# Pooled attention and two MLPs on one core: sums and conversions held in program order, the first attention along the weight fold, y from other tiles

## The chip, the cores and the metric

The kernel runs on one core of one Trainium2 chip. Its engines are TensorE (PE in the profile; PEld is its weight load), VectorE (DVE), ScalarE (ACT), GpSimd (POOL) and SyncE (SP), each working through its own stream of instructions in order. The metric is the time of one execution on the device in microseconds; the median of three runs counts.

## The reference

All inputs of the two MLPs are float64 words in DRAM, q, k and v are float32. What is computed, cut to what matters:

```python
# attention: 8 batches, 8 heads, 576 tokens, 64 wide; k and v averaged over 8 tokens
k_p = k.reshape(B, H, 72, 8, D).mean(axis=3)
v_p = v.reshape(B, H, 72, 8, D).mean(axis=3)
attn = softmax(q @ k_p.T / sqrt(D))
x = (attn @ v_p) as (4608 tokens, 512)
# first MLP (512 -> 1024 -> 1024 -> 512)
x = ((x @ w1) * (x @ w2)) @ w3 @ w_out
# second MLP (512 -> 1536 -> 512), after a norm
xn = x / sqrt(mean(x * x) + 1e-6) * rms_g
y = (silu(xn @ w_gate) * (xn @ w_val)) @ moe2_w_out
```

## The kernel before

The 4608 tokens are handled in nine blocks of 512 (index i), the attention in eight batches of 576 tokens (index b), so that a batch ends inside a block. Matrix products run as three passes over a high and a low part of each operand (`mm3`, L104 to L106; `split`, L100 and L101).

The program has these stages. First the **fold**: w3 · w_out of the first MLP is multiplied out once. Sixteen steps n, each with four transposes of a block of w3 (L553), ScalarE's copy of the transposed block into `hl` (L555) and four products (L622). The float64 words are turned into float32 by a `Conv`: a load (`s0`), then ScalarE takes the low word (L143) and, if `on_act`, the high one (L145), VectorE shifts it (L154), merges the sign (L159) and adds the two (L167). `conv.run` issues conversion steps up to a count; each step of the fold calls it for the next block, two steps more than needed. Within the fold, the attention of batch 0 and the first products `ab(0, m, s)` are called from a list `aux` that a `Ticker` spreads over the products behind number `AUX_FROM`.

Then come seven more batches of attention beside the products `ab` of blocks 0 to 8 (x·w1, copied by ScalarE at L567, times x·w2 by VectorE at L570) and beside `gv_prep`, which converts the weights of the second MLP into sums of blocks (L774) and high and low parts (`wst`, L100 and L101), stored by POOL (L791). `positions(b)` lays the steps of a batch over sixteen places: place 1 the load of the next batch's k (`k0`), 8 the sum of v, 9 the next batch's loads of v, 13 the products with v, 14 the sum of the next batch's k (`k1`), 15 its transpose (`kT`, L282) and first q transposes (L301). `pool_four` loads half of each group of 8 tokens by SP (L243) and lets POOL's DMA add the other half (L244); `pool_sum` adds the four that are left on VectorE (L248, then L251). Scores are L319, their maximum L331 on VectorE, the exponential L334 on ScalarE, the division L345 to L347 on VectorE; the transposes of the result go over TensorE (L369) in the first two batches and over VectorE (L362) in the others; the product with v is L422, and its high and low parts are written by L429 (ScalarE) and L430 (VectorE, `xl`).

Behind them the products with the folded matrix give y; `y_end` squares y (L700), copies it into a tile `yc` (L703, L705) for the store to DRAM (L706) and adds the squares (L708, split at L714 and L716) for the norm. The second MLP (`gv`, g·silu at L1015 to L1019, x scaled in `xprep`, L1051) and its last products into `y`, `o` fill the rest.

The code is written in one order, but a scheduler places each engine's instructions by its own estimate of their times, within what data and buffers allow. So an engine's stream can differ from the program. Tiles come from rings: `ftile` has five, `hxtile("hh")` and `hxtile("hl")` two each; a ring's next tile waits for the last use of the one that it takes over. The functions that the change touches:

Of the kernel before, what the change touches and what calls it, by code (L numbers as in the profile page):

```python
# [9 lines left out]
F32 = mybir.dt.float32  # L10
# [4 lines left out]
ALU = mybir.AluOpType  # L15
# [6 lines left out]
def kernel(  # L22
# [86 lines left out]
    class Conv:  # L109
# [19 lines left out]
        def s1(self):  # L129
# [13 lines left out]
            nc.scalar.activation(self.low, low_u, AF.Copy, scale=2.0**-29)  # L143
            if self.on_act:
                nc.scalar.activation(self.tmp.bitcast(F32), hi_f, AF.Copy, scale=2.0**-112)  # L145
            else:
                nc.vector.tensor_scalar(
                    out=self.tmp.bitcast(F32),
                    in0=hi_f,
                    scalar1=2.0**-112,  # L150
                    scalar2=None,
                    op0=ALU.mult,
                )
            nc.vector.tensor_scalar(  # L154
                out=self.tmp, in0=self.tmp, scalar1=3, scalar2=None, op0=ALU.logical_shift_left
            )

        def s2(self):
            nc.vector.scalar_tensor_tensor(  # L159
                out=self.low,  # L160
                in0=self.hiw,
                scalar=-(2**31),
                in1=self.low,
                op0=ALU.bitwise_and,
                op1=ALU.bitwise_or,
            )
            nc.vector.tensor_tensor(out=self.out, in0=self.tmp, in1=self.low, op=ALU.add)  # L167
# [79 lines left out]
    def pool_sum(dst, r):  # L247
        nc.vector.tensor_tensor(  # L248
            out=r[:, :, : 2 * D], in0=r[:, :, : 2 * D], in1=r[:, :, 2 * D :], op=ALU.add
        )  # L250
        nc.vector.tensor_tensor(  # L251
            out=dst,
            in0=r[:, :, :D].rearrange("s (p j) d -> s p j d", j=2),
            in1=r[:, :, D : 2 * D].rearrange("s (p j) d -> s p j d", j=2),
            op=ALU.add,
        )
# [280 lines left out]
    def load_w3(n):  # L537
        g, j = divmod(n, KF1)

        def keep(f):  # L540
            w3r[n] = f

        src = w3.rearrange("(g i p) c -> g p i c", g=2, p=P)[g, :, :, j * P : (j + 1) * P]
        return Conv(src, praw, then=keep)
# [4 lines left out]
    def tr_w3(n):  # L549
        ps = psum()  # L550
        r = w3r.pop(n)
# [44 lines left out]
    first = {5: [A.k0], 6: [A.load_v], 7: [lambda: A.q(0)], 8: [lambda: A.q(1)]}  # L596
# [5 lines left out]
    aux += [atts[1].k0, atts[1].load_v, lambda: atts[1].q(0)]  # L602
    for m in range(4):
        aux += [lambda m=m: ab(0, m, 0), c1a[m], lambda m=m: ab(0, m, 1)]
    aux += c1a[4:]
    aux += [atts[1].k1, lambda: atts[1].q(1)]
    AUX_FROM = 38
    tick = Ticker(aux, 4 * NW3 - AUX_FROM)
    conv.run(upto[0] + 2)
    tr_w3(0)  # L610
    wps = None
    for n in range(NW3):
        g, j = divmod(n, KF1)
        if n + 1 < NW3:
            conv.run(upto[n + 1] + 2)
# [23 lines left out]
    tick.flush()  # L639
    nc.sync.dma_start(out=g_col, in_=rms_g.rearrange("(k p) -> p k", p=P))  # L640


    def y_end(i):
        ys = yacc.pop(i)
        sq = []
        for kk in range(KD):
            sq.append(ftile())
            nc.scalar.activation(sq[kk], ys[kk], AF.Square)
            yc = ftile()
            if kk % 2:  # L650
                nc.scalar.copy(yc, ys[kk])
            else:
                nc.vector.tensor_copy(yc, ys[kk])
            nc.sync.dma_start(out=ydram[i, kk], in_=yc)
            if kk:
                nc.vector.tensor_tensor(out=sq[0], in0=sq[0], in1=sq[kk], op=ALU.add)

        sp = []

        def sq_split():  # L660
            sp.append(ftile(F32R))
            nc.scalar.copy(sp[0], sq[0])
            sp.append(ftile(F32R))
            nc.vector.tensor_tensor(
                out=sp[1], in0=sq[0], in1=sp[0].bitcast(F32), op=ALU.subtract
            )

        def rms():
            ps = psum()
            nc.tensor.matmul(ps[:1], ones, sp[0], start=True, stop=False)  # L670
            nc.tensor.matmul(ps[:1], ones, sp[1], start=False, stop=True)
            row = ftile()
            nc.scalar.copy(row[:1], ps[:1])
            nc.sync.dma_start(out=sdram[i : i + 1], in_=row[:1])
            ss = const.tile([P, 4], F32, tag="ss", name="ss", bufs=2)
            nc.sync.dma_start(out=ss, in_=sdram[i].rearrange("(p c) -> p c", p=P))
            nc.vector.tensor_scalar(
                out=ss, in0=ss, scalar1=1.0 / DM, scalar2=1e-6, op0=ALU.mult, op1=ALU.add
            )
            nc.gpsimd.tensor_tensor(out=ss, in0=ss, in1=mhalf, op=ALU.pow)  # L680
            nc.sync.dma_start(out=rdram[i].rearrange("(p c) -> p c", p=P), in_=ss)

        return [sq_split, lambda: None, rms]

    def y_mm(i, m):
        c = m % 4
        second(i, m, wph[m // 4][:, c, :], wpl[m // 4][:, c, :], KF1 - 1, False)
        return y_end(i) if m == KF1 - 1 else []
# [6 lines left out]
    def y_end(i):  # L695
        ys = yacc.pop(i)
        sq = []
        for kk in range(KD):
            sq.append(ftile())
            nc.scalar.activation(sq[kk], ys[kk], AF.Square)  # L700
            yc = ftile()
# [323 lines left out]
    def xprep(i0):  # L1025
# [21 lines left out]
        def norm(j, u):  # L1047
            for k in range(2):
                z = q[f"A{j + 1}{u + 1}"][:, k * TB : (k + 1) * TB]
                kk = 2 * u + k  # L1050
                nc.vector.scalar_tensor_tensor(  # L1051
                    out=z,
                    in0=z,
                    scalar=g_col[:, kk : kk + 1],
                    in1=rr["r"][:, j * TB : (j + 1) * TB],
                    op0=ALU.mult,
                    op1=ALU.mult,
# [301 lines left out]
```

## Time and profile before

| What | us |
|---|---|
| median of three runs | 1726.54 |
| lowest, highest | 1725.12, 1729.22 |
| the profiled execution | 1726.03 |
| its span | 1724.3 |
| TensorE busy | 1622.2 |
| VectorE busy | 1012.9 |
| ScalarE busy | 679.7 |
| POOL busy | 95.0 |

The span is what the profile covers of the execution; the remaining 1.7 us lie around it. A line of waits names the engine and line that waited, what it waited for, the time in all, how many waits, and the longest. A line of the timeline gives the start, the duration, the engine and its instruction, and in brackets the idle time ahead of it with what ended it. PEclk is the share of TensorE's full clock that was granted.

### The profile page before, as it was taken

The page shows a single profiled execution, that of the slowest core. Times are in us where ns is not written, and L with a number is a line of the kernel's source. Part 1 is how long each engine was busy: PE and PEld are TensorE (multiplying, and loading weights), DVE is VectorE, ACT ScalarE, POOL GpSimd, SP SyncE. Part 2 cuts the span into 40 slices and gives each one's busy share as a digit, 9 for nine tenths or more (in the row PEclk, how much of TensorE's full clock was granted, in tenths as well). Part 3 has the DMA queues.
Part 4 walks back from the last instruction along what each step waited for, and adds up shares of the span by engine and source line. Part 5 has one row for each costly group of instructions (what it writes and reads, how often), then busy time and mean ns, then how long its engine had stood idle before and what let it go on. Part 6 is the DMA issues. An engine that isn't in the chain of part 4 may idle for free.

```text
span 1724.3 us, 20001 instructions
## 1 busy us (share of the span) xinstructions
PE 1622.2 (94%) x7250; PEld 1295.7 (75%) x7250; DVE 1012.9 (59%) x1773; ACT 679.7 (39%) x1607; POOL 95.0 (6%) x107
## 2 busy tenths in 40 slices
PE   6787997897988999999998999999999999999999
PEld 3445776675866778888876888888888888888887
DVE  6565586886967941566483242567354744465344
ACT  5675543444444431455441133333333333234322
POOL 0101011011011010001000000000000000000000
PEclk9898998998989999999999999999999999999999
DMA  8958447475574256577655664547454745455431
GB/s 244 255 138 207 122 125 180 150 172 156 151 176 156 98 189 244 194 251 255 210 202 192 228 259 169 195 183 266 149 220 169 272 182 193 160 208 197 183 109 74
DMA packets 147461, 322.53 MB, mean 187 GB/s; under 512 B 52505, under 2 KB 79129, under 8 KB 129442
## 3 DMA queue, kind: packets, MB, share of 16 engines
q1 hardware_dynamic: 126210, 276.13, 47.4%
q0 software_dynamic: 21152, 45.12, 10.0%
q8 instruction: 57, 0.93, 0.2%
q14 instruction: 42, 0.34, 0.1%
HBM read 247.75 MB, written 73.44 MB: 186 GB/s over the span
## 4 chain that ended last, share of the span: by engine, by line
PE 72%; DMA 11%; DVE 10%; issue 6%; ACT 1%; POOL 1%; SPq 1%; POOLq 0%; DVEq 0%; ACTq 0%
PE ps L104 14%; PE ps L106 14%; PE ps L105 14%; DMA kv<-in_k_dram 5%; PE o L106 5%; PE o L105 5%; PE o L104 5%; DVE aT L362 5%; PE y L104 4%; PE y L106 4%; PE y L105 4%; DMA kv<-in_v_dram 3%; PE pa L319 1%; DMA q<-in_q_dram 1%; PE wps L622 1%
## 5 line engine op out<-in xcount | busy, mean ns | idle before, releaser
L104 PE MATMUL ps<-xf,wr 128*128 128x512 f32 x576 | 224.2, 389 | 0.0
L105 PE MATMUL ps<-xf,wr 128*128 128x512 f32 x576 | 224.1, 389 | 0.0
L106 PE MATMUL ps<-xf,wr 128*128 128x512 f32 x576 | 224.1, 389 | 0.0
L106 PE MATMUL o<-oh,hcl 128*128 128x512 f32 x384 | 149.5, 389 | 0.0
L105 PE MATMUL o<-ol,hch 128*128 128x512 f32 x384 | 149.4, 389 | 0.0
L104 PE MATMUL o<-oh,hch 128*128 128x512 f32 x384 | 149.4, 389 | 0.0
L1117 ACT COPY f<-ps 128x512 f32<-128x512 f32 x144 | 84.4, 586 | 161.8 <-PE ps L106 158.6
L362 DVE STREAM_TRANSPOSE aT<-s 32x256 f32<-32x256 f32 x324 | 140.8, 435 | 4.5
L104 PEld LDWEIGHTS ps<-xf,wr 128*128 128x128 f32 x576 | 108.1, 188 | 23.0 <-ACT f L1117 0.4
L105 PEld LDWEIGHTS ps<-xf,wr 128*128 128x128 f32 x576 | 108.1, 188 | 22.5
L106 PEld LDWEIGHTS ps<-xf,wr 128*128 128x128 f32 x576 | 108.1, 188 | 22.2
L104 PE MATMUL ps<-xh,w1h 128*128 128x512 f32 x288 | 123.6, 429 | 1.0 <-ACT w1h L100 1.0
L1121 DVE TENSOR_TENSOR f<-y,f 128x512 f32<-128x512 f32 x48 | 33.2, 691 | 144.4 <-PE y L106 144.4
L334 ACT ACTIVATE s<-pa,mx 128x72 f32<-128x72 f32 (+1 forms) x280 | 85.3, 331 | 82.7 <-DVE mx L331 82.6
L105 PE MATMUL ps<-xl,w1h 128*128 128x512 f32 x288 | 116.5, 404 | 0.0
L106 PE MATMUL ps<-xh,w1l 128*128 128x512 f32 x288 | 116.1, 403 | 0.2 <-DVE w1l L101 0.2
L104 PE MATMUL ps<-xh,w2h 128*128 128x512 f32 x288 | 113.9, 396 | 2.1 <-DVE hh L570 1.8
L106 PE MATMUL ps<-xh,w2l 128*128 128x512 f32 x288 | 112.3, 390 | 0.0
L105 PE MATMUL ps<-xl,w2h 128*128 128x512 f32 x288 | 112.0, 389 | 0.0
L1203 DVE TENSOR_TENSOR acc<-o,acc 128x512 f32<-128x512 f32 x64 | 43.5, 689 | 75.5 <-PE o L106 75.0
L1141 ACT CAST hch<-f 128x512 fp32r<-128x512 f32 x72 | 44.8, 622 | 99.9 <-DVE f L1135 99.9
L106 PEld LDWEIGHTS o<-oh,hcl 128*128 128x128 f32 x384 | 72.1, 188 | 15.3 <-DVE hcl L1143 0.6
(194 smaller groups left out, 3268.9 us busy)
## 6 DMA issues: line engine op xcount, KB each, us to landing
wr<-wd SPq DMA_DIRECT2D x96, 1024.0 KB
wd<-wst POOLq DMA_DIRECT2D x48, 512.0 KB, 5.6
hr<-hd SPq DMA_DIRECT2D x36, 512.0 KB
oh<-od SPq DMA_DIRECT2D x15, 1024.0 KB
ol<-od SPq DMA_DIRECT2D x15, 1024.0 KB
wr<-wd SPq DMA_DIRECT2D x24, 512.0 KB
x1raw<-in_moe_w_dram SPq DMA_DIRECT2D x20, 512.0 KB
hd<-hh SPq DMA_DIRECT2D x40, 256.0 KB
```

What stands on the lines that cost most here:

```text
L104: nc.tensor.matmul(o, lh, rh, start=first, stop=False, skip_group_check=part)
L105: nc.tensor.matmul(o, lh, rl, start=False, stop=False, skip_group_check=part)
L106: nc.tensor.matmul(o, ll, rh, start=False, stop=last, skip_group_check=part)
L319: nc.tensor.matmul(ps[:n, (p % 2) * 2 * SP : (p % 2 + 1) * 2 * SP], qT_t[t // 2][:, t % 2, p, :n], kT[:, p, :], start=True, stop=True,)
L334: nc.scalar.activation(s_t[t][:n, h, :SP], pv[:, j, :], AF.Exp, bias=mx[:, j, :], accum_out=den_t[t][:n, h, :],)
L362: nc.vector.transpose(aT[32 * kb : 32 * kb + 32, :, s0 + 32 * i : s0 + 32 * i + 32], s_t[t][32 * i : 32 * i + 32, :, 32 * kb : 32 * kb + 32],)
L622: nc.tensor.matmul(wps[i], wt[:, i * P : (i + 1) * P], wo[j // 4][:, j % 4, :], start=j == 0, stop=j == KF1 - 1,)
L1117: nc.scalar.copy(t, bank)
L1121: nc.vector.tensor_tensor(out=t, in0=bank, in1=t, op=ALU.add)
L1141: nc.scalar.copy(hi, hf)
L1203: nc.vector.tensor_tensor(out=a, in0=ys[j], in1=a, op=ALU.add)
```

## The change

Four things change.

1. `tc.keep_in_program_order` is put around four instructions: the first addition of `pool_sum`, ScalarE's low word of a conversion (L143), VectorE's merge (L159) and the scaling of x in `xprep` (L1051). Such an instruction is placed behind the instruction that stood ahead of it on its engine in the program; no wait is added. The shift (second half of L154) is called behind the merge.
2. The blocks of w3 are read through their `Conv` instead of a callback, and the fold asks for one conversion step ahead instead of two.
3. Batch 0's loads are called at the fold's steps 0 to 3 instead of 5 to 8, its attention from product 18 on instead of 38, and `ab(0, 0..3)` with their conversions behind the fold (`tail`).
4. `y_end` copies y into `hh` and `hl` tiles. (An earlier, overwritten copy of `y_end` and `y_mm` is deleted as well.)

```diff
-            nc.scalar.activation(self.low, low_u, AF.Copy, scale=2.0**-29)
+            tc.keep_in_program_order(
+                nc.scalar.activation(self.low, low_u, AF.Copy, scale=2.0**-29)
+            )
...
+        def s2(self):
+            tc.keep_in_program_order(
+                nc.vector.scalar_tensor_tensor(
+                    out=self.low,
...
+            )
             nc.vector.tensor_scalar(
                 out=self.tmp, in0=self.tmp, scalar1=3, scalar2=None, op0=ALU.logical_shift_left
             )
...
     def pool_sum(dst, r):
-        nc.vector.tensor_tensor(
-            out=r[:, :, : 2 * D], in0=r[:, :, : 2 * D], in1=r[:, :, 2 * D :], op=ALU.add
+        tc.keep_in_program_order(
+            nc.vector.tensor_tensor(
+                out=r[:, :, : 2 * D], in0=r[:, :, : 2 * D], in1=r[:, :, 2 * D :], op=ALU.add
+            )
         )
...
-        return Conv(src, praw, then=keep)
+        w3r[n] = Conv(src, praw)
+        return w3r[n]
...
-        r = w3r.pop(n)
+        r = w3r.pop(n).out.bitcast(F32)
...
-    first = {5: [A.k0], 6: [A.load_v], 7: [lambda: A.q(0)], 8: [lambda: A.q(1)]}
+    first = {0: [A.k0], 1: [A.load_v], 2: [lambda: A.q(0)], 3: [lambda: A.q(1)]}
...
+    tail = [c1a[0]]
     for m in range(4):
-        aux += [lambda m=m: ab(0, m, 0), c1a[m], lambda m=m: ab(0, m, 1)]
-    aux += c1a[4:]
-    aux += [atts[1].k1, lambda: atts[1].q(1)]
-    AUX_FROM = 38
+        tail += [lambda m=m: ab(0, m, 0), c1a[m + 1], lambda m=m: ab(0, m, 1)]
+    tail += [c1a[5], atts[1].k1, lambda: atts[1].q(1)]
+    AUX_FROM = 18
...
-            conv.run(upto[n + 1] + 2)
+            conv.run(upto[n + 1] + 1)
...
     tick.flush()
+    for st in tail:
+        st()
...
-            yc = ftile()
+            yc = hxtile("hh" if kk % 2 else "hl").bitcast(F32)
...
-                nc.vector.scalar_tensor_tensor(
-                    out=z,
...
+                tc.keep_in_program_order(
+                    nc.vector.scalar_tensor_tensor(
+                        out=z,
```

Where instructions stand now is shown at three places. The first is VectorE's stream where batch 5 begins (`kv_3305` is a half of the k of batch 6, `xl5_3259` the low part of block 5's x, `vp_3559` the summed v, the 128x320 piece being the first). Before:

```order
L570 TENSOR_TENSOR hl_3256<-ps_3243,f_3241 128x512
L248 TENSOR_TENSOR kv_3305<-kv_3305 72x4x128
L430 SCALAR_TENSOR_TENSOR xl5_3259<-pa_3260,xh5_3258 128x320
L430 SCALAR_TENSOR_TENSOR xl5_3259<-pa_3265,xh5_3258 128x320
L430 SCALAR_TENSOR_TENSOR xl5_3259<-pa_3270,xh5_3258 128x320
L251 TENSOR_TENSOR vp_3559<-kv_3032 72x256
L430 SCALAR_TENSOR_TENSOR xl5_3259<-pa_3275,xh5_3258 128x320
L331 TENSOR_REDUCE mx_3283<-pa_3280 128x4
L331 TENSOR_REDUCE mx_3283<-pa_3297 128x4
L251 TENSOR_TENSOR vp_3559<-kv_3035 72x256
L159 SCALAR_TENSOR_TENSOR rawp_3454<-rawp_3454 128x512
L251 TENSOR_TENSOR kv_3305<-kv_3305 72x2x128
```

And now, where the sum of the same tile stands (the 128x192 pieces are the last of the block; the four 128x320 pieces stand some 60 rows ahead, with no sum of `kv_3305` beside them):

```order
L574 TENSOR_TENSOR hl_3704<-ps_3691,f_3680 128x512
L436 SCALAR_TENSOR_TENSOR xl5_3259<-pa_3706,xh5_3258 128x192
L436 SCALAR_TENSOR_TENSOR xl5_3259<-pa_3711,xh5_3258 128x192
L436 SCALAR_TENSOR_TENSOR xl5_3259<-pa_3716,xh5_3258 128x192
L436 SCALAR_TENSOR_TENSOR xl5_3259<-pa_3721,xh5_3258 128x192
L253 TENSOR_TENSOR kv_3305<-kv_3305 72x4x128
L168 TENSOR_SCALAR f_3688<-f_3688 128x512
L257 TENSOR_TENSOR kv_3305<-kv_3305 72x2x128
L253 TENSOR_TENSOR kv_3308<-kv_3308 72x4x128
L574 TENSOR_TENSOR hh_3765<-ps_3752,f_3740 128x512
L257 TENSOR_TENSOR kv_3308<-kv_3308 72x2x128
```

The sum of `kv_3305` moved from ahead of block 5's first xl to behind its last one.

The second place is TensorE's stream in the fold, around the fold's eighth to eleventh block (L553 a block's transposes, L622 its products, L282 and L301 the first of batch 0's attention). Before:

```order
L553 MATMUL ps<-ident,f 128x128 x4
L622 MATMUL wps<-wo,hl 128x512 x4
L553 MATMUL ps<-ident,f 128x128 x4
L622 MATMUL wps<-wo,hl 128x512 x4
L553 MATMUL ps<-ident,f 128x128 x4
L622 MATMUL wps<-wo,hl 128x512 x4
L553 MATMUL ps<-ident,f 128x128 x4
L622 MATMUL wps<-wo,hl 128x512
L282 MATMUL ps<-ident,kv 128x72 x4
L301 MATMUL ps<-ident,q 128x128 x4
```

And now, around the sixth and seventh block (L557, L626, L288, L307 and L325 are the L553, L622, L282, L301 and L319 of before):

```order
L557 MATMUL ps<-ident,f 128x128 x4
L626 MATMUL wps<-wo,hl 128x512 x4
L288 MATMUL ps<-ident,kv 128x72 x2
L307 MATMUL ps<-ident,q 128x128 x4
L288 MATMUL ps<-ident,kv 128x72 x2
L307 MATMUL ps<-ident,q 128x128 x4
L626 MATMUL wps<-wo,hl 128x512
L557 MATMUL ps<-ident,f 128x128 x4
L325 MATMUL ps<-kT,qT 128x144 x2
L307 MATMUL ps<-ident,q 128x128 x4
L626 MATMUL wps<-wo,hl 128x512
L325 MATMUL ps<-kT,qT 128x144 x2
```

Attention's first transposes moved from behind the eleventh block to behind the sixth.

The third place is VectorE's stream where the second MLP's products begin, with what each instruction waits for (L1016 and L1019 the steps of silu, L716 the low part of the squares' sum, `hl<-f,hh` the low part for the last products). Before:

```order
L1016 TENSOR_TENSOR f<-ps,f 128x512 [waits Activation_49]
L1016 TENSOR_TENSOR f<-ps,f 128x512 [waits DMAHW0_49,Activation_49]
L716 TENSOR_TENSOR f<-f 128x512 [waits DMAHW6_49,DMAHW4_49,Activation_49]
L1019 TENSOR_TENSOR f<-ps,f 128x512 [waits DVE_49,PE_49] x2
L101 TENSOR_TENSOR hl<-f,hh 128x512 [waits Activation_49] x2
L1016 TENSOR_TENSOR f<-ps,f 128x512 [waits Activation_49] x2
```

And now (L975, L675 and L978 are the L1016, L716 and L1019 of before):

```order
L975 TENSOR_TENSOR f<-ps,f 128x512 [waits Activation_49]
L975 TENSOR_TENSOR f<-ps,f 128x512 [waits DMAHW0_49,Activation_49]
L675 TENSOR_TENSOR f<-f 128x512 [waits PE_49,Activation_49]
L978 TENSOR_TENSOR f<-ps,f 128x512 [waits DVE_49,PE_49]
L101 TENSOR_TENSOR hl<-f,hh 128x512 [waits DMAHW1_49,Activation_49]
L978 TENSOR_TENSOR f<-ps,f 128x512 [waits PE_49]
L101 TENSOR_TENSOR hl<-f,hh 128x512 [waits DMAHW4_49,Activation_49]
```

L716's wait for two DMA queues is gone, the split into `hl` has one each, and the scaling of x moved behind this place.

## Rows read from the trace of the kernel before

**Rows 1.** The page, section 1: busy us, share of the span, instructions.
```profile
PE 1622.2 (94%) x7250; PEld 1295.7 (75%) x7250; DVE 1012.9 (59%) x1773; ACT 679.7 (39%) x1607; POOL 95.0 (6%) x107
```

**Rows 2.** Windows: stretch, length, busy PE, PEld, DVE, ACT, POOL; clock, DMA, GB/s.
```profile
0.00:63.00 63.00, 43.88 (x121) 21.03 (x122) 40.49 (x78) 35.01 (x59) 7.29 (x14) 0.97 0.90 245
63.00:148.00 85.00, 72.32 (x300) 45.49 (x299) 54.05 (x105) 54.42 (x159) 4.96 (x4) 0.92 0.66 182
148.00:604.00 456.00, 396.82 (x1955) 315.91 (x1956) 352.34 (x792) 208.55 (x798) 58.17 (x64) 0.93 0.57 152
604.00:896.00 292.00, 292.00 (x1289) 238.37 (x1286) 153.48 (x201) 120.56 (x170) 22.16 (x24) 1.00 0.64 219
896.00:920.00 24.00, 17.02 (x67) 13.54 (x66) 12.07 (x20) 6.82 (x11) 1.38 (x1) 0.86 0.69 248
```

**Rows 3.** Waits of PE, 148 to 604: us in all, times, longest.
```profile
PE pa L319 <- DVE xl L430: 23.1, 4, 8.9
...
PE pa L301 <- DVE xl L430: 9.1, 3, 8.1
...
PE pa L282 <- DVE xl L430: 8.8, 4, 2.8
PE pa L369 <- DVE s L347: 8.5, 1, 8.5
```

**Rows 4.** Waits of DVE in the same stretch.
```profile
DVE kv L248 <- DMA kv<-in_k_dram: 45.2, 10, 9.3
...
DVE rawp L159 <- ACT rawp L143: 11.9, 5, 5.6
...
DVE kv L248 <- DMA kv<-in_v_dram: 5.9, 2, 3.6
```

**Rows 5.** Timeline, 418 to 420: start, us, engine, instruction, idle before it.
```profile
418.58 0.69 DVE L248 TENSOR_TENSOR kv<-kv 72x512 f32<-72x512 f32 x1 [9.31 <-DMA kv<-in_k_dram]
419.19 1.28 DVE L430 SCALAR_TENSOR_TENSOR xl<-pa,xh 128x320 fp32r<-128x320 f32 x3
...
419.73 0.61 PE L319 MATMUL pa<-kT,qT 128*128 128x144 f32 x1 [8.88 <-DVE xl L430]
```

**Rows 6.** Chain that ended last, 380 to 440: start, us, what.
```profile
405.41 13.15 DMA kv<-in_k_dram
```

**Rows 7.** Windows behind that hold.
```profile
418.00:421.00 3.00, 1.27 (x5) 1.26 (x6) 2.42 (x6) 0.66 (x1) 0.00 (x0) 0.50 0.75 156
421.00:424.00 3.00, 3.00 (x13) 2.71 (x12) 1.66 (x5) 2.06 (x9) 0.00 (x0) 0.50 0.53 121
424.00:427.00 3.00, 3.00 (x14) 2.43 (x13) 2.93 (x8) 2.00 (x12) 0.62 (x1) 0.91 0.38 105
```

**Rows 8.** Timeline of DVE and of PE where another batch ends.
```profile
331.48 2.67 DVE L362 STREAM_TRANSPOSE aT<-s 32x256 f32<-32x256 f32 x6
334.18 0.69 DVE L570 TENSOR_TENSOR hl<-ps,f 128x512 f32<-128x512 f32 x1
334.79 1.67 DVE L430 SCALAR_TENSOR_TENSOR xl<-pa,xh 128x320 fp32r<-128x320 f32 x4
...
335.32 0.47 PE L282 MATMUL pa<-ident,kv 72*128 72x72 f32 x4 [2.50 <-DVE xl L430]
```

**Rows 9.** Waits of ACT, 148 to 604.
```profile
ACT rawp L143 <- DMA rawp<-in_moe_w_val_dram: 19.6, 6, 6.9
...
ACT rawp L143 <- DMA rawp<-in_moe_w_gate_dram: 15.4, 5, 5.1
```

**Rows 10.** Waits of PE, 0 to 148.
```profile
PE wps L622 <- ACT hl L555: 10.5, 4, 4.9
PE ps L553 <- DVE f L167: 6.9, 1, 6.9
PE ps L369 <- DVE s L347: 6.1, 1, 6.1
```

**Rows 11.** Chain that ended last, 0 to 700: two of its DMAs.
```profile
43.99 8.19 DMA x1raw<-in_moe_w_dram
...
55.26 13.36 DMA q<-in_q_dram
```

**Rows 12.** Timeline where the last products begin.
```profile
909.46 0.69 DVE L716 TENSOR_TENSOR f<-f 128x512 fp32r<-128x512 f32 x1 [3.84 <-issue]
...
911.65 0.80 PE L104 MATMUL y<-oh,hh 128*128 128x512 f32 x1 [6.98 <-ACT hh L100]
```

More of the change, by code (lines that the diff above doesn't have):

```diff
@@ L153, in s1 @@
                 )
+        def s2(self):
+            tc.keep_in_program_order(
+                nc.vector.scalar_tensor_tensor(
+                    out=self.low,
+                    in0=self.hiw,
+                    scalar=-(2**31),
+                    in1=self.low,
+                    op0=ALU.bitwise_and,
+                    op1=ALU.bitwise_or,
+                )
+            )
             nc.vector.tensor_scalar(
                 out=self.tmp, in0=self.tmp, scalar1=3, scalar2=None, op0=ALU.logical_shift_left
-            )
-        def s2(self):
-            nc.vector.scalar_tensor_tensor(
[L160 to L165, printed above, removed]
             )
@@ L247, in pool_sum @@
     def pool_sum(dst, r):
-        nc.vector.tensor_tensor(
-            out=r[:, :, : 2 * D], in0=r[:, :, : 2 * D], in1=r[:, :, 2 * D :], op=ALU.add
+        tc.keep_in_program_order(
+            nc.vector.tensor_tensor(
+                out=r[:, :, : 2 * D], in0=r[:, :, : 2 * D], in1=r[:, :, 2 * D :], op=ALU.add
+            )
         )
@@ L538, in load_w3 @@
         g, j = divmod(n, KF1)
-        def keep(f):
-            w3r[n] = f
         src = w3.rearrange("(g i p) c -> g p i c", g=2, p=P)[g, :, :, j * P : (j + 1) * P]
-        return Conv(src, praw, then=keep)
+        w3r[n] = Conv(src, praw)
+        return w3r[n]
     def load_wo(j):
@@ L602 @@
     aux += [atts[1].k0, atts[1].load_v, lambda: atts[1].q(0)]
+    tail = [c1a[0]]
     for m in range(4):
-        aux += [lambda m=m: ab(0, m, 0), c1a[m], lambda m=m: ab(0, m, 1)]
-    aux += c1a[4:]
-    aux += [atts[1].k1, lambda: atts[1].q(1)]
-    AUX_FROM = 38
+        tail += [lambda m=m: ab(0, m, 0), c1a[m + 1], lambda m=m: ab(0, m, 1)]
+    tail += [c1a[5], atts[1].k1, lambda: atts[1].q(1)]
+    AUX_FROM = 18
     tick = Ticker(aux, 4 * NW3 - AUX_FROM)
-    conv.run(upto[0] + 2)
+    conv.run(upto[0] + 1)
     tr_w3(0)
@@ L639 @@
     tick.flush()
+    for st in tail:
+        st()
     nc.sync.dma_start(out=g_col, in_=rms_g.rearrange("(k p) -> p k", p=P))
[L643 to L648, printed above, removed]
-            yc = ftile()
[L650 to L688, printed above, removed]
     def ybank(i):
@@ L700, in y_end @@
             nc.scalar.activation(sq[kk], ys[kk], AF.Square)
-            yc = ftile()
+            yc = hxtile("hh" if kk % 2 else "hl").bitcast(F32)
             if kk % 2:
@@ L1050, in norm @@
                 kk = 2 * u + k
-                nc.vector.scalar_tensor_tensor(
-                    out=z,
[L1053 to L1057, printed above, removed]
+                tc.keep_in_program_order(
+                    nc.vector.scalar_tensor_tensor(
+                        out=z,
+                        in0=z,
+                        scalar=g_col[:, kk : kk + 1],
+                        in1=rr["r"][:, j * TB : (j + 1) * TB],
+                        op0=ALU.mult,
+                        op1=ALU.mult,
+                    )
                 )
```

## Prediction

> **What bounds the kernel now.** I read the page's shares and slices first, then the busy time by stage, then the waits of the one stage that has gaps, then the timeline at one of its waits, and last the start and the change to the last products.
>
> TensorE is busy for 94% of the span, so the whole gain that is open lies in its gaps [rows 1]. By stage [rows 2]: 43.9 + 72.3 of the first 148 us (fold and first attention), 396.8 of the 456 us from 148 to 604 (seven batches of attention beside the first products), 292.0 of 292.0 us up to 896, 17.0 of 24 us where the last products begin. The gaps are 31.8, 59.2, 0 and 7.0 us. An edit pays only in the first, the second and the fourth stage.
>
> In the second stage the idle time of TensorE has one releaser: xl at L430 (23.1 + 9.1 + 8.8 us) and the scaled s at L347 (8.5 us), together 49.5 of 59.2 us, both written by VectorE [rows 3]. VectorE in turn waited 45.2 + 5.9 = 51.1 us at L248, the first addition of a sum of k or v, for the DMA of k or v [rows 4]. The two sums are, but for 2 us, the same microseconds. One place shows how: an accumulating load of k took 13.15 us from 405.41 [rows 6]; L248, which waits for it, held VectorE for 9.31 us, the L430 behind it in the order were already due, and TensorE started 1.15 us after L248 with 8.88 us lost [rows 5]. The scheduler had put a sum that is needed one batch later ahead of the xl that is needed at once.
>
> The granted clock goes down with such a hold: 0.50 from 418 to 424, the lower of the levels 1.2 and 2.4 GHz, and 0.91 up to 427 [rows 7]. TensorE worked there for 1.27 + 3.00 + about 0.5 us at half speed, a loss of 2.4 us behind a wait of 8.88 us, or 0.27 us for each. For 49.5 us that is 13 us as the upper bound; I take 11, since the shorter of the 12 waits need not bring it down, and 4 as the lower bound (the two waits of this length).
>
> **The change part by part.** The sum is made against the profiled execution, 1726.03 us with a span of 1724.3; the median of the runs is 1726.54, so the difference counts for nothing.
>
> *Sums of k and v.* L248 now stands where the program has it, behind the last xl of the previous batch. In the order of VectorE the sum of tile kv_3305, which stood directly ahead of xl5's first piece, now stands behind xl5's last one, some 70 instructions later. For every batch from the second on, at least 71 VectorE instructions lie between the result that POOL's queue waits for ahead of the accumulating DMA and the sum; before it was 3 to 27 for most. At 0.44 us of busy time for one (352.34 us by 792) [rows 2] that is 31 us, against the 13.15 us that the transfer above took [rows 6]. So the waits at L248 go, and with them 49.5 us of TensorE's. No instruction is added. What is queued behind the sum if it should wait all the same: the same xl, now of the next batch.
> What is late next is VectorE itself. Without the holds TensorE's floor in this stage is 396.8 − 11 = 386 us, and VectorE has 352 us of work for it, 91%. One place shows what that means: at 335.32 TensorE waited 2.50 us for xl though VectorE had not stood still at all [rows 8]. I leave 2.5 us for each of seven batch ends, 17.5 us, and 4 us for the conversions below. Gain: 49.5 + 11 − 21.5 = 39, say 40 us; bounds 59 + 11 = 70 (all idle time gone) and 49.5 + 4 − 43 = 11 (twice those 21.5 us, the low bound of the clock).
>
> *Conversion steps.* L143 on ScalarE and the merge L159 on VectorE hold their place in the program; the shift L154 goes behind the merge. The instructions are the same in number. In before, the scheduler placed them, and they waited for their words all the same: ScalarE 19.6 us in 6 waits and 15.4 in 5 for w_val and w_gate [rows 9], VectorE 11.9 us in 5 for ScalarE [rows 4]. A place held in order may be worse: a wait for one load then stops everything behind it, exp L334 on ScalarE, xl on VectorE. The trace doesn't show the pinned order, so the bounds are: at best the 11.9 us go, at worst each of the 28 conversions of this stage waits as long as ScalarE's mean wait of 35.0/11 = 3.2 us, 28 × 3.2 − 11.9 = 78 us (24 of w_gate and w_val, 4 of w2's last ones). I take a loss of 4 us (in the sum above), nearest to the rows of VectorE, since ScalarE is busy for less than half of the stage (208.55 of 456) and waits there without TensorE.
>
> *First batch along the fold.* The loads of k, v and q of batch 0 come at steps 0 to 3 instead of 5 to 8, its attention runs from the sixth of the 16 fold steps instead of the eleventh, and the four products ab(0, 0 to 3), which stood among its last pieces, follow behind the fold. The first 148 us have 31.8 us of gaps; 6.9 lie ahead of the first transpose [rows 10], so 24.9 are open. The largest of the rest are waits of the fold for its transposed block (L622 for ScalarE's hl, 10.5 us) and of attention for s (6.1) [rows 10]; work of the one beside the other, from the sixth step on, fills both. The other side is the DMA: share 0.90 at 245 GB/s in the first 63 us and 182 GB/s up to 148 [rows 2], 15.4 + 15.5 = 30.9 MB, at 245 GB/s 126 us. So no more than 22 us can be gained by order alone. Below: half of k and all of v and q of batch 0 (2.9 MB by their shapes) may now stand ahead of words of w3, 12 us by the same rate, and ready attention must cover that; if it covers half, 6 us are lost. I take 16 us, two thirds of what is open, between −6 and 22, since a wait that stands ahead of the sixth step (the longest for hl, 4.9 us, is in step 0) is not reached, and each attention piece still waits for its own softmax.
> A q load of batch 0 took 13.36 us where 512 KB of w took 8.19 [rows 11]. The Trainium skill, page "DMA: Bandwidth & Descriptors", section "Specifications", asks for at least 512 B for the full rate and says that less makes the engine read, modify and write; a row of q has 256 B. By that, as an estimate from that page, the 1.18 MB of the first batch's q cost twice their bytes while the queues are full, some 4.8 us at 245 GB/s, which would give 11 instead of 16 us here and 1671 in all. The rows above agree in direction, and I don't take the figure.
>
> *y from h tiles, xprep in order.* yc no longer takes a tile of the five-deep f ring, so L716 doesn't wait for a y store; the h splits now do. From 604 to 896 TensorE is never idle, and the h tiles are hardly used there, so this costs nothing. At the start of the last products TensorE waited 6.98 us for hh; VectorE's L716 had been held for 3.84 us ahead of the L1019 that hh needs [rows 12]. At a clock of 0.86 over 24 us [rows 2], part of it idle, some 2 us more are lost. Of these 9 I take 4: hh itself now waits for a y store that was issued a few us before. Bounds 9 (all of it) and −4 (hh waits for its store as long as L716 now does, on top).
>
> Sum: 16 + 40 + 4 = 60 us, 1726 − 60 = **1666 us**.
>
> **The rivals.**
> *Everything goes.* All gaps that were named are filled: 22 + 70 + 9 = 101 us, 1625. For it: the holds have one cause. Against it: VectorE at 91% of TensorE's time.
> *Half.* VectorE becomes the bound in the second stage (one wait for xl at every piece, not at every batch), the gain there is 20, in the first 7, at the turn 0: 1699. For it: 2.50 us of wait without any hold [rows 8]; the merges now stand between transposes and xl. Against it: over the stage VectorE stood still 104 us.
> *The pinned steps hold.* A conversion's load is issued when its buffer comes free, with its merge close behind in program order. If each of the 28 held VectorE and with it TensorE for the 3.2 us of ScalarE's mean wait, that is 78 us in place of the 4 in the sum: 1666 + 74 = 1740, slower. It decides from (60 + 4 + 11.9)/28 = 2.7 us per conversion. For it: [rows 9], and an order that can't step aside. Against it: only 11.9 of ScalarE's 35 us of waits reached VectorE.
> *The sums wait in their new place too*, since POOL's queue is behind wst stores, and the fold gains nothing: 1715 to 1730. Against it: 71 instructions of distance.
>
> **How the numbers follow.** Forecast (1645 to 1685) 0.52, everything goes (1620 to 1645) 0.12, half (1685 to 1715) 0.22, no gain 0.04 (1715 to 1730), held 0.10. The range leaves out the last two cases and a small part of the outermost: 1630 to 1710. The measurement tells 0.2%, 3.5 us, from no change. Faster 0.86, same 0.04, slower 0.10.
>
> **What would show it.** Right: VectorE's waits at L248 between 148 and 604 under 10 us (51.1 now), TensorE's for xl and s under 25 (49.5), no stretch of clock 0.50 as from 418 to 424; the first product of batch 1's stage some 16 us earlier than 148; the wait of 6.98 halved. Wrong: long waits of VectorE at L159 for L143 with TensorE behind; waits for the words of w3 in the fold that grow by more than attention fills; a VectorE without gaps and a TensorE with many small ones (half).

## The result, and the profile after

Before 1727.59 us, after 1677.81 us (medians of four runs each, for before one run more than in the table ahead); the ratio is 0.9712, with an interval of 0.969 to 0.9734. The forecast was 1666 us in a range of 1630 to 1710: 60 us less were forecast, 50 came. The sum was nearly right, but not the terms for the first stretch and for the conversion steps, as the experiments show.

The profiled execution has a span of 1673.2 us. Three marks divide it: the first transposes of batch 1's k (148.1 us before, 143.9 after), the last product with v (603.03 and 557.30), and the first of the last products y (911.65 and 863.70). The stretches went from 148.1 to 143.9, from 454.9 to 413.4, from 308.6 to 306.4, and from 812.7 to 809.5. So 4.2, 41.5, 2.2 and 3.2 us are gone, 51.1 in all; the forecast's terms were 16 for the first stretch, 40 for the second and 4 for the last two.

The windows of the kernel after, to be read beside [rows 2] (length, busy time of PE, PEld, DVE, ACT, POOL with instructions, granted clock, DMA share, GB/s):

```profile
0.00:63.00 63.00, 43.13 (x136) 22.21 (x137) 35.46 (x71) 34.78 (x79) 6.08 (x12) 0.92 0.89 234
63.00:144.00 81.00, 73.68 (x289) 43.42 (x287) 57.15 (x108) 54.19 (x141) 7.25 (x8) 0.96 0.79 235
144.00:557.00 413.00, 383.49 (x1949) 305.33 (x1947) 353.47 (x788) 206.96 (x793) 56.10 (x60) 0.97 0.59 161
...
563.00:850.00 287.00, 287.00 (x1254) 234.96 (x1253) 132.66 (x180) 109.62 (x159) 19.14 (x21) 0.99 0.63 216
850.00:870.00 20.00, 20.00 (x89) 16.53 (x89) 8.23 (x13) 7.95 (x13) 1.01 (x1) 1.00 0.71 263
```

In the second stage TensorE is idle for 413 − 383.5 = 29.5 us in place of 59.2, and the clock is 0.97 in place of 0.93. Between the two marks themselves (before, then after) the 41.5 us are idle time, 59 to 30 us, and busy time, 12 us less for the same products:

```profile
148.08:603.03 454.95, 395.77 (x1950) 315.50 (x1948) 351.29 (x790) 208.47 (x798) 57.31 (x62) 0.92 0.57 153
143.91:557.30 413.39, 383.58 (x1949) 305.42 (x1948) 353.77 (x791) 207.11 (x794) 56.10 (x60) 0.97 0.59 161
```

VectorE does the same work, 353 us, now in 413 us (86%, before 77%). The window of the last products has no idle time left, where [rows 12] showed 6.98 us.

TensorE's waits in the second stage after, to be read beside [rows 3]:

```profile
PE pa L288 <- issue: 15.4, 5, 5.3
PE ps L105 <- DVE xl L436: 8.1, 3, 3.1
PE pa L428 <- ACT kT L293: 2.9, 1, 2.9
```

VectorE's four longest in the same stretch, beside [rows 4]:

```profile
DVE f L168 <- ACT f L147: 15.5, 5, 5.6
DVE mx L337 <- PE pa L325: 9.4, 14, 1.6
DVE den L351 <- ACT s L340: 8.2, 4, 2.1
DVE wst L101 <- ACT wst L100: 6.1, 2, 3.2
```

No line for a sum of k or v stands there any more (51.1 us before), and none for a merge. The conversions' waits are not gone, though: the longest line is the shift (L168) behind the merge, which waits 15.5 us for ScalarE's high word; before, merge and shift together waited 11.9 + 7.5 = 19.4 us. What is left of TensorE's waits is a chain that starts from VectorE's own backlog. One of the five waits of L288 (the timeline of TensorE and of VectorE at the end of a batch; L436 is xl, L253 and L257 the sums of k):

```profile
306.27 0.69 DVE L574 TENSOR_TENSOR hl<-ps,f 128x512 f32<-128x512 f32 x1
306.88 1.67 DVE L436 SCALAR_TENSOR_TENSOR xl<-pa,xh 128x320 fp32r<-128x320 f32 x4
308.47 0.68 DVE L253 TENSOR_TENSOR kv<-kv 72x512 f32<-72x512 f32 x1
309.07 0.42 DVE L168 TENSOR_SCALAR f<-f 128x512 int32<-128x512 int32 x1
309.41 0.41 DVE L257 TENSOR_TENSOR kv<-kv 72x256 f32<-72x256 f32 x1
...
309.92 0.47 PE L288 MATMUL pa<-ident,kv 72*128 72x72 f32 x2 [5.34 <-issue]
```

VectorE has no idle bracket there. The sum is no longer ahead of xl; it is behind it, and nothing waits for a DMA. The profile names no releaser for L288 (`issue`); that it waits for the sum is read from the times, as here L257 ends at 309.82 and L288 starts 0.10 us later.

### The profile page after: what moved, and what is told of

Its sections match the earlier page's. It is cut to its first block, busy times and chain, and to the rows that moved or that the text cites. A ratio compares the mean times of both kernels' runs of the same rounds, so it can differ in the third digit from the quotient of the medians.

```text
span 1673.2 us, 19957 instructions
## 1 busy us (share of the span) xinstructions
PE 1612.5 (96%) x7250; PEld 1285.4 (77%) x7250; DVE 1012.9 (61%) x1773; ACT 680.6 (41%) x1607; POOL 93.5 (6%) x107
## 4 chain that ended last, share of the span: by engine, by line
PE 81%; DVE 10%; DMA 4%; issue 2%; ACT 2%; SPq 0%; DVEq 0%; ACTq 0%
PE ps L104 16%; PE ps L105 16%; PE ps L106 16%; PE o L106 5%; PE o L105 5%; PE o L104 5%; DVE aT L368 5%; PE y L106 4%; PE y L104 4%; PE y L105 4%; DMA x1raw<-in_moe_w_out_dram 2%; PE pa L428 2%; PE pa L325 1%; PE wps L626 1%; PE pa L307 1%
## 5 line engine op out<-in xcount | busy, mean ns | idle before, releaser
L368 DVE STREAM_TRANSPOSE aT<-s 32x256 f32<-32x256 f32 x324 | 140.8, 435 | 4.6
L104 PE MATMUL ps<-xh,w1h 128*128 128x512 f32 x288 | 119.7, 416 | 0.0
L104 PEld LDWEIGHTS o<-oh,hch 128*128 128x128 f32 x384 | 72.1, 188 | 15.0
```

Source lines behind the costliest of these rows:

```text
L104: nc.tensor.matmul(o, lh, rh, start=first, stop=False, skip_group_check=part)
L368: nc.vector.transpose(aT[32 * kb : 32 * kb + 32, :, s0 + 32 * i : s0 + 32 * i + 32], s_t[t][32 * i : 32 * i + 32, :, 32 * kb : 32 * kb + 32],)
```

## The experiments

Times are medians; before ran 1724.28, 1723.17, 1723.87 and 1724.07 us on the chips of the four groups, so kernels of different groups are compared by their ratio to it. The kernel after was measured beside 1727.59: its distance to the others in microseconds of the medians is some 3 to 5 us off that of the ratios (0.001 is 1.7 us). Where two intervals overlap, the difference is not told from none. The marks and waits come from one profiled execution of each kernel.

| Kernel | median us | ratio, interval | first mark | second | third | span |
|---|---|---|---|---|---|---|
| before | 1727.59 | 1 | 148.1 | 603.0 | 911.7 | 1724.3 |
| after | 1677.81 | 0.9712, 0.969 to 0.9734 | 143.9 | 557.3 | 863.7 | 1673.2 |
| sums alone | 1668.76 | 0.9687, 0.9653 to 0.9721 | 134.3 | 546.0 | 853.5 | 1666.0 |
| after, sums free | 1694.28 | 0.9832, 0.9801 to 0.9862 | 142.7 | 578.5 | 880.0 | 1690.2 |
| after, conversions free | 1667.01 | 0.9665, 0.963 to 0.97 | 141.6 | 556.2 | 857.7 | 1667.5 |
| after, old fold | 1664.01 | 0.9655, 0.9622 to 0.9687 | 138.3 | 546.2 | 852.5 | 1662.0 |
| old fold, loads early | 1666.11 | 0.9661, 0.9637 to 0.9686 | 141.5 | 548.5 | 854.9 | 1664.4 |
| old fold, one step ahead | 1678.28 | 0.9734, 0.971 to 0.9758 | 153.3 | 560.5 | 866.9 | 1676.4 |
| sums and y alone | 1665.94 | 0.9663, 0.9629 to 0.9697 | 139.0 | 550.3 | 853.2 | 1666.8 |
| after, two steps ahead | 1670.39 | 0.9686, 0.9657 to 0.9715 | 138.5 | 553.2 | 859.9 | 1669.4 |
| old fold, conversions free | 1663.89 | 0.965, 0.9621 to 0.9679 | 139.7 | 553.0 | 854.5 | 1664.2 |
| old fold, k's sum early | 1664.46 | 0.9658, 0.9634 to 0.9682 | 140.8 | 549.3 | 854.2 | 1663.7 |
| old fold, y from f tiles | 1669.72 | 0.97, 0.9666 to 0.9733 | 138.0 | 544.3 | 854.2 | 1665.7 |
| old fold, three steps ahead | 1662.18 | 0.9645, 0.9628 to 0.9661 | 136.8 | 542.8 | 849.3 | 1658.7 |

**Sums alone** (on the kernel before).

```diff
     def pool_sum(dst, r):
-        nc.vector.tensor_tensor(
...
+        tc.keep_in_program_order(
+            nc.vector.tensor_tensor(
...
```

> The kernel before with one edit: the first addition of a sum of k or v holds its place in program order. Theory (the holds at that addition are the second stage's loss): of the 1727 us some 40 go, 1682 to 1692, VectorE's waits at that addition between the stage's ends under 10 us in place of 51, TensorE's waits for xl and s under 25. Rival (the conversion steps held in order are what took VectorE's holds away): 1715 or more, and the waits move to the conversion's merge.

It came out below the range: 55.5 us are gone by the medians, as much as the whole change brings or more (0.9687 and 0.9712, intervals that overlap). In the second stage 412 us are left of 454.9, 43 less, near the 40 that were forecast. Another 14 us are in the first: it ends at 134.3 in place of 148.1 (at 139.0 in the kernel with sums and y below, whose first stretch has the same edits, so 9 to 14 us). There VectorE had waited 19.6 and 4.6 us for v and k, which the forecast had not listed (before, 0 to 148, VectorE):

```profile
DVE kv L248 <- DMA kv<-in_v_dram: 19.6, 4, 8.5
...
DVE kv L248 <- DMA kv<-in_k_dram: 4.6, 2, 3.9
```

With the sums alone 0.4 us for k are left of these among VectorE's waits of the first 134 us. The rival falls: the conversion steps were free here.

**After, sums free.** The pin around the sum is taken out of the changed kernel.

```diff
     def pool_sum(dst, r):
-        tc.keep_in_program_order(
-            nc.vector.tensor_tensor(
...
+        nc.vector.tensor_tensor(
...
```

> The changed kernel with the sums of k and v left to the scheduler again. Theory: the holds come back, 1678 + 40 = 1710 to 1722, VectorE waits 40 us and more for the DMA of k and v. Rival (conversion steps): under 1690.

16.5 us are lost by the medians (21 by the ratios), less than expected, though the holds are back at 38 us of VectorE's time in the second stage (between 143 and 578):

```profile
DVE kv L252 <- DMA kv<-in_k_dram: 24.2, 10, 5.1
...
DVE kv L252 <- DMA kv<-in_v_dram: 13.6, 6, 2.8
```

The stage is 22 us longer than in the changed kernel (435.8 and 413.4), and the stretch behind it 5 us shorter. So the pin does what was said, but its worth depends on what else is changed: 55 us alone, 16 to 21 beside the other edits, which without it take 30 us off the kernel before, 19 of them in the second stage. The first stretch ends at 142.7, no later than in the changed kernel (143.9), though VectorE waits 17.6 us for k and v in it: beside the moved fold no gain of the pin shows there. The time lies between the numbers of the theory and of the rival.

**After, conversions free.**

```diff
-            tc.keep_in_program_order(
-                nc.scalar.activation(self.low, low_u, AF.Copy, scale=2.0**-29)
-            )
+            nc.scalar.activation(self.low, low_u, AF.Copy, scale=2.0**-29)
...
-        def s2(self):
-            tc.keep_in_program_order(
```

> The changed kernel with the conversion steps (ScalarE's low word, VectorE's merge) free and the shift ahead of the merge again. Theory (they are no part of the gain): 1674 to 1684; if the in-order merges cost the first stage its missing gain (VectorE waited 23.9 us at the merge for ScalarE there, 14.5 before), 1664 to 1672. Rival (they gave the gain): 1700 or more.

1667.01 us, inside the range that was given for a cost of the merges. But the place is another: the two first marks differ by little (556.2 and 557.3 at the second), and 4.9 us lie between the second and the third mark. There, in the changed kernel, the last xl comes late, and the clock goes to its lower level for the work behind it. The windows of the changed kernel from 553, and then those of this one from 552:

```profile
553.00:557.00 4.00, 0.88 (x4) 0.38 (x3) 3.91 (x10) 0.00 (x0) 0.00 (x0) 1.00 0.00 0
557.00:561.00 4.00, 3.70 (x10) 1.07 (x12) 3.42 (x8) 3.06 (x4) 1.26 (x2) 0.62 0.17 66
561.00:565.00 4.00, 4.00 (x11) 1.56 (x8) 2.60 (x5) 1.22 (x3) 1.68 (x3) 0.50 0.95 321
565.00:569.00 4.00, 4.00 (x12) 3.10 (x12) 0.16 (x1) 0.16 (x1) 0.00 (x0) 0.60 1.01 294
```

```profile
552.00:556.00 4.00, 3.05 (x14) 2.20 (x12) 3.90 (x11) 0.53 (x1) 0.00 (x0) 1.00 0.06 24
556.00:560.00 4.00, 3.77 (x17) 1.25 (x18) 4.00 (x9) 3.61 (x7) 1.93 (x4) 1.00 0.35 127
560.00:564.00 4.00, 4.00 (x18) 3.30 (x18) 3.11 (x6) 1.66 (x3) 1.00 (x2) 1.00 0.97 318
564.00:568.00 4.00, 4.00 (x19) 3.31 (x18) 1.12 (x2) 0.01 (x1) 0.00 (x0) 1.00 0.99 292
```

The changed kernel waited 3.42 us for xl with the merge L159 and the addition L171 ahead of it among VectorE's transposes; this one waited 1.17 us and kept its clock. At (0.38, 0.50, 0.40) × 4 us the clock alone costs 1.5 + 2.0 + 1.6 = 5.1 us. But the pinned steps alone don't make this wait: with the sums free the merge and the addition stand at the same place (572.36 and 573.33), and TensorE waited 1.30 us. The last products with v in the changed kernel, in this one and in the one with the sums free:

```profile
557.30 6.50 PE L428 MATMUL pa<-aT,vp 72*64 72x512 f32 x16 [3.42 <-DVE xl L436]
556.23 3.65 PE L424 MATMUL pa<-aT,vp 72*64 72x512 f32 x16 [1.17 <-DVE xl L432]
578.47 3.65 PE L426 MATMUL pa<-aT,vp 72*64 72x512 f32 x16 [1.30 <-DVE xl L434]
```

From the division of the last batch (L353, L349 and L351, at 550.52, 550.64 and 571.70) to these products it is 6.8, 5.6 and 6.8 us, so the merge and the addition cost 1.2 us; the rest is that VectorE came to the division later, 3.4, 4.4 and 5.5 us before TensorE ran out of products. Why it did was not tried. The profiled executions differ by 5.7 us in all, the medians by 10.8 and the ratios by 8, with intervals that overlap.

**After, old fold.** The fold's calls are as in the kernel before, everything else as after.

```diff
-    first = {0: [A.k0], 1: [A.load_v], 2: [lambda: A.q(0)], 3: [lambda: A.q(1)]}
+    first = {5: [A.k0], 6: [A.load_v], 7: [lambda: A.q(0)], 8: [lambda: A.q(1)]}
...
-    tail = [c1a[0]]
     for m in range(4):
-        tail += [lambda m=m: ab(0, m, 0), c1a[m + 1], lambda m=m: ab(0, m, 1)]
-    tail += [c1a[5], atts[1].k1, lambda: atts[1].q(1)]
-    AUX_FROM = 18
+        aux += [lambda m=m: ab(0, m, 0), c1a[m], lambda m=m: ab(0, m, 1)]
+    aux += c1a[4:]
+    aux += [atts[1].k1, lambda: atts[1].q(1)]
+    AUX_FROM = 38
...
-    conv.run(upto[0] + 1)
+    conv.run(upto[0] + 2)
...
-            conv.run(upto[n + 1] + 1)
+            conv.run(upto[n + 1] + 2)
...
     tick.flush()
-    for st in tail:
-        st()
```

> The changed kernel with the fold's calls as before: loads of batch 0 at steps 5 to 8, its attention from product 38 on, the first products among it, two conversion steps ahead. Theory (moving the first batch is worth the 4 us by which the first stage became shorter): 1680 to 1684, the first transposes of batch 1 at about 148. Rival (the move costs as much in late words of w3 as it gives, and the 4 us come from elsewhere): 1672 to 1678.

Both missed: it is 13.8 us faster than the changed kernel by the medians, 10 by the ratios. The changed fold as a whole, which had been forecast to bring 16 us, costs 10 to 14 beside the other edits. The first mark is 5.6 us earlier without it, the second 11.1. (The reading of w3 through its `Conv` stays in all these kernels and was never tried alone.)

**Which part of the fold costs.** The next two put one part of it into the old fold each, and the third takes one out of the changed kernel. First the early loads:

```diff
-    first = {5: [A.k0], 6: [A.load_v], 7: [lambda: A.q(0)], 8: [lambda: A.q(1)]}
+    first = {0: [A.k0], 1: [A.load_v], 2: [lambda: A.q(0)], 3: [lambda: A.q(1)]}
```

> The changed kernel with the fold's calls as before (e4_old_fold), but batch 0's loads of k, v and q called at the fold's steps 0 to 3. Theory (the loads stand ahead of words of w3 and w_out, whose last block of w_out was asked for at 43.5 us in the changed kernel and at 32.8 with the old fold): the first stage ends 4 to 8 us later than with the old fold's 138.3, time 1668 to 1674. Rival (what costs is the look-ahead of one step less, or the first products that follow the fold instead of filling it): 1660 to 1667, as the old fold.

1666.11 us. The first mark comes 3.2 us later, the median 2.1 us; with intervals of 0.9637 to 0.9686 and 0.9622 to 0.9687 that is no difference that can be told, and the rival's range holds. The loads in front of w3's words were the suspect; with the old fold they are nearly free.

Then the look-ahead of the conversion steps:

```diff
-    conv.run(upto[0] + 2)
+    conv.run(upto[0] + 1)
...
-            conv.run(upto[n + 1] + 2)
+            conv.run(upto[n + 1] + 1)
```

> The old fold (e4_old_fold) with one conversion step ahead instead of two. Theory (the early loads cost): 1660 to 1667. Rival (the look-ahead costs: each conversion starts one step later, with its load behind): 1668 to 1676, more wait of TensorE for the transposed block and the converted words in the first 120 us.

1678.28 us, 14.3 more than the old fold, on the rival's side and 2 us above its range: with the old fold, one step of look-ahead costs as much as the whole of the fold's change. The first mark is at 153.3 in place of 138.3. One wait makes it (timelines of VectorE and TensorE in this kernel; `raw` are words of w2, `x1raw` the last block of w3):

```profile
112.56 0.69 DVE L159 SCALAR_TENSOR_TENSOR raw<-raw 128x512 int32<-128x512 int32 x1 [0.72 <-ACT raw L144]
...
116.64 0.69 DVE L159 SCALAR_TENSOR_TENSOR raw<-raw 128x512 int32<-128x512 int32 x1 [1.72 <-ACT raw L144]
...
118.92 0.69 DVE L159 SCALAR_TENSOR_TENSOR x1raw<-x1raw 128x512 int32<-128x512 int32 x1
119.64 0.69 DVE L171 CUSTOM_DVE_ANT_0 f<-x1raw,f 128x1024 uint16<-128x1024 uint16 x1
...
120.48 1.09 PE L557 MATMUL ps<-ident,f 128*128 128x128 f32 x4 [14.37 <-DVE f L171]
```

The merge of the fold's last block stands behind merges of w2 whose low words waited for their loads (ScalarE's L144, 6.2 us in five waits between 90 and 125), since merges keep the program's order and the program asks for that block one step later. With two steps ahead the same transposes start at 103.45 without a wait. That it takes the pinned merges as well is read from this order: the old fold with one step ahead and free conversions was not run. The changed kernel, with one step ahead and other calls around it, has no wait of this length: 6.8 us is the longest at L557 with the conversions pinned, 6.9 us at its L553 with them free.

And the changed kernel with two steps:

> The changed kernel with two conversion steps ahead in the fold, as before. Theory (early loads cost): 1674 to 1680, no better than the changed kernel. Rival (look-ahead): 1666 to 1672, and the first stage ends at 136 to 140 instead of 143.9.

1670.39 us: 7.4 us of the 13.8 come back by the medians, 4.5 of 10 by the ratios, with intervals that overlap; the first mark is at 138.5, 5.4 us earlier, as the rival had it. The remaining 4 to 6 us against the old fold are in the early loads, in the attention from product 18 on and in the first products behind the fold; the last two were not tried alone. Against the old fold with early loads (1666.11 us) it is 4.3 us slower, with the second mark 4.7 us later.

**Three steps ahead** (old fold, `+ 2` to `+ 3`).

> The old fold (e4_old_fold) with three conversion steps ahead instead of two. Theory (the fold waits for its converted words, and a step more of look-ahead brings them earlier; from one step to two the first stage fell from 153.3 to 138.3): 1656 to 1662, the first stage ends by 134. Rival (two steps are enough: the wait of 14.37 us for the last block's words was the whole effect, and it is gone): 1662 to 1667.

1662.18 us, 0.9645 against 0.9655 for two steps: no difference that can be told, though the first mark is 1.5 us and the second 3.3 us earlier, and the time lies at the edge between the two ranges. Two steps are about enough. It is the lowest median of the study: the interval of its ratio (0.9628 to 0.9661) lies below that of the changed kernel.

**Old fold, conversions free.**

> The old fold (e4_old_fold), with the conversion steps free and the shift ahead of the merge: sums and x scaling in order, y from h tiles. Theory (conversion steps in order cost some us, as without them the changed kernel fell from 1677.8 to 1667.0): 1656 to 1661. Rival (they cost only where the look-ahead is one step, since a load is then asked for too late for the place that is held): 1662 to 1668.

1663.89 us, no difference to the old fold (1664.01). The rival holds: with two steps ahead the pinned conversion steps cost nothing in sum. The marks show two parts that cancel: the second is 6.9 us later without the pins (5.5 of them in the second stage, 413.3 in place of 407.9 us), the stretch behind it 4.9 us shorter, since the last xl comes in time and the clock stays up as above.

**Sums and y alone** (on the kernel before: the pin around the sum, and `yc` from `hh` and `hl` tiles).

```diff
-            yc = ftile()
+            yc = hxtile("hh" if kk % 2 else "hl").bitcast(F32)
```

> The kernel before with two edits: the sums of k and v in program order and y copied into h tiles. Theory (the y edit takes away the wait of 6.98 us at the first of the last products and its half clock, and nothing else): 6 to 9 us less than with the sums alone (1668.8), 1658 to 1664, with the rest of the trace as there. Rival (the wait goes because the scaling of x was held in order): 1665 to 1670, the wait of some 6 us stays.

1665.94 us against 1668.76 with the sums alone, intervals that overlap by most; neither theory is told apart by the times. The trace tells more. The wait for hh at the first of the last products is 5.86 us with the sums alone and 1.21 us here; but from the second mark to the end it is 820.0 and 816.5 us, so of the 9 us that were open 3.5 came. Of the rest 2.75 us went to a new wait, for a load of weights 7 us later (the first line is of the sums alone, the others of this kernel):

```profile
853.46 0.79 PE L104 MATMUL y<-oh,hh 128*128 128x512 f32 x1 [5.86 <-ACT hh L100]
...
853.17 0.50 PE L104 MATMUL y<-oh,hh 128*128 128x512 f32 x1 [1.21 <-ACT hh L100]
860.13 0.50 PE L104 MATMUL ps<-xnh,wr 128*128 128x512 f32 x1 [2.75 <-DMA wr<-wd]
```

(The first mark differs by 4.7 us between the two kernels, where nothing was changed: so much can the first stretch of one execution differ by itself.)

**Old fold, y from f tiles.** The same edit undone in the kernel with the old fold, with the scaling of x still in order:

> The old fold (e4_old_fold) with y copied into f tiles as before, the scaling of x still in order. Theory (the y edit alone takes the wait at the first of the last products away): the wait for hh of some 6 us and the half clock behind it come back, 1669 to 1674. Rival (the scaling of x held in order, which no longer stands ahead of those products, does it): 1660 to 1666, no wait there.

1669.72 us, 5.7 more than with h tiles, in intervals that overlap. The wait for hh is back at 1.61 us, not 6, with the clock at 0.86 behind it:

```profile
854.17 0.50 PE L104 MATMUL y<-oh,hh 128*128 128x512 f32 x1 [1.61 <-ACT hh L100]
...
852.00:864.00 12.00, 10.39 (x38) 7.77 (x37) 3.35 (x5) 1.75 (x3) 0.00 (x0) 0.86 0.59 232
```

So each edit takes a part of the wait: with x in order and without the y edit 1.61 us are left, with the y edit and without x in order 1.21 us, with both none, whether the conversions are pinned or free. The time lies in the theory's range, the trace agrees with neither side alone.

**Old fold, k's sum early.** The last wait of the second stage was tried on: the sum of the next batch's k is called at place 11 instead of 14.

```diff
-            pos[14] += [C.k1, lambda: C.q(1)]
+            pos[11] += [C.k1]
+            pos[14] += [lambda: C.q(1)]
```

> The old fold (e4_old_fold) with the sum of the next batch's k at place 11 instead of 14. Theory (what is left in the second stage is VectorE's backlog at a batch's end: TensorE waits 15.4 us in 5 for the sums behind the last xl, 8 in 3 for xl): the waits for the transposes of k fall under 5 us, 1648 to 1657. Rival (the same work only moves on VectorE, and the next late thing is xl): 1660 to 1667, the waits for xl grow by what those of the transposes lose.

1664.46 us, no difference. The rival holds to the microsecond: with the sum behind xl TensorE waited 15.4 us for the transposes of k and 8.0 for xl (old fold), now it waits 24.0 us for xl alone (TensorE's waits of the old fold, then of this kernel, in the second stage):

```profile
PE pa L288 <- issue: 15.4, 5, 5.3
PE ps L105 <- DVE xl L436: 8.0, 3, 3.1
```

```profile
PE pa L288 <- DVE xl L436: 24.0, 5, 5.6
```

What is late at a batch's end in these two kernels is VectorE as a whole, whatever stands last.

## Why the prediction was right, and where it was not

**The mechanism of the second stage was right, and its size.** The two sums that were the same microseconds, VectorE's at L248 and TensorE's for xl and s, went together: 51.1 and 49.5 us to none and to a rest of another kind. Forecast 40 us, measured 41.5 (47 with the old fold, 43 with the sums alone). The distance of 71 instructions was enough, since no sum waits for its DMA there. Forecast for the rest were 21.5 us of lateness of VectorE beside the 9.7 us outside the named waits, 31 in all; 29.5 us of idle time are left, 23.5 of them in waits for xl and for the sums behind it. Of the 41.5 us that came, 29 are idle time (49.5 − 21.5 = 28 forecast) and 12 are TensorE's busy time for the same products, with the granted clock at 0.97 in place of 0.92: the 11 us that were taken for the clock. One sign of being right was not met: stretches at 0.50 are left, from 309 to 315, from 432 to 438 and behind the last xl.

**The step that failed is the first batch along the fold,** 16 us. Measured 4.2 us in the first stretch, and beside the other edits even these are not the move's: with the sums alone the first stretch is 9 to 14 us shorter, and beside the pinned sums the changed fold makes it 5.6 us longer and the second stage another 5.5. (Without the pinned sums the rest of the change shortens the first stretch by 5.4 us; the two don't add up.) Two omissions made it. First, the rows of TensorE's waits for its transposed block and for s were read without asking what VectorE waited for at that time, as had been done one stage later: the row for the sums of v (19.6 us) was there, and the same edit takes it away. Secondly, the look-ahead, `+ 2` to `+ 1`, which stands in the diff, was given no price at all. It costs 14.3 us in the old fold; in the changed kernel the first stretch is 5.4 us longer by it, and the 4.5 to 7.4 us in the time are not clear of the noise.

**The bound that speaks of DMA** (early loads in front of w3's words, 12 us) was too high, where it was tried: with the old fold the first mark came 3.2 us later, and the 2.1 us in the median are not told from none. No run tests the estimate of 4.8 us from the Trainium skill, page "DMA: Bandwidth & Descriptors", section "Specifications": the rows of q have 256 B in every kernel here, and the one difference that bears on it, 2.1 us, lies within intervals that reach some 4 us to either side.

**The conversion steps** were forecast to lose 4 us in waits, and the slower rival had them at 74 us more. In the second stage itself nothing was lost: it takes 413.4 us with the pins and 414.7 without, with the old fold 407.9 and 413.3. The waits moved from the merge to the shift behind it (19.4 us of both before, 15.5 after). What was lost lies elsewhere: once, behind the last xl, 5 us by the clock, and only beside pinned sums; and together with the short look-ahead, where a held merge stood behind others' loads and TensorE waited 14.37 us (in the old fold). That looks like the rival's mechanism, an order that can't step aside, at one place, not at 28. In the changed kernel 10.8 us lie between the pinned and the free conversions by the medians, 8 by the ratios, with intervals that overlap.

**The turn to the last products** was forecast at 4 us in a bound of −4 to 9; 5.4 us came behind the second mark, and that is after the loss of about 5 us of clock right behind it. So the edits of y and x gave some 9 to 10 us, all of the bound; with the conversions free, where that loss is absent, the two stretches behind the second mark take 811.3 us, 10 less than before and 8.7 less than with the sums alone.

**The total came near in part by luck: two errors cancel in part.** Left out: the sums in the first stretch, 9 to 14 us too little. Wrongly counted: 16 us for the fold, which costs 10 to 14 in total. The rival "half" had the right mechanism for what is left, VectorE as the bound, but its price for the second stage was not reached.

## What to carry to other kernels

When an engine's stream waits for a transfer, look for what that instruction was needed for: a sum needed a batch later had been placed ahead of work needed at once, and fixing its place gave more by itself than the rest of the change by itself (55.5 and 30 us). Apply that question to every stretch of the trace, not only to the one with the longest waits. Check a pin and a look-ahead together: behind an instruction that is held in order, everything waits for its load, and with the merges pinned one step less of lead made a wait of 14 us. When the last wait of a stage is one engine's backlog, moving one of its instructions only renames the wait.

## What the runs showed of the hardware

The granted clock fell behind waits that were short. At the last products with v TensorE waited 3.4 us in the eight kernels with both the sums and the conversions pinned, and in the first 4 us behind that wait the clock was at 0.57 to 0.68, in the next 4 us at 0.50, the lower of its levels of 1.2 and 2.4 GHz: 5.1 us of work lost in the changed kernel, more than the wait itself. In the six others, before among them, TensorE waited 1.17 to 1.53 us there, and the clock stayed at 1.00. A wait shortened by 2.25 us was so worth some 7, as an estimate from these two numbers.

The length of the wait does not decide it alone. At the last products a wait of 1.61 us (old fold, y from f tiles) was followed by 0.89, 0.50 and 0.76 in the stretches of 2 us from 854, and one of 2.75 us (sums and y) by 1.00 throughout.
